# Four raw weight buffers in the first layer, a smaller descriptor reserve, and two conversion steps placed later

## The chip, the cores and the metric

The kernel runs on one core of a Trainium2 chip. The metric is device time in microseconds; the comparison is between medians of several runs. The core has a matrix engine (PE, with its weight loads shown as PEld), a vector engine (DVE), an activation engine (ACT), a general engine (POOL) and a sync engine (SP), which here issues all DMA transfers. Each engine works through its own instructions in order.

## What is computed

Three stages in float32, of which each feeds the next: causal attention with a decay, a layer with the activation h·cos(h), and a gated layer with silu.

```python
scores = scale * q @ k^T + (cum[:, None] - cum[None, :])   # causal, 32 heads of 576 x 64
x = softmax(scores) @ v                                    # then 2304 tokens x 512
h = x @ w_in;  x = (h * cos(h)) @ w_out                    # w_in 512 x 2048, w_out 2048 x 512
g = x @ w_gate; x = (silu(g) * (x @ w_val)) @ w_out2       # 512 x 1536, 1536 x 512
```

The five weight matrices arrive as float64 bit patterns (the kernel sees pairs of 32-bit words), so they have to be turned into float32 on the chip before a matmul can use them. A float32 operand is then split into a high and a low part, and three matmuls replace one.

## The kernel before

**Attention** runs over 16 pairs of heads. The order of its steps is written out by hand in the string `SCH`: each token is an operation and, behind the @, by how many rounds it lags. The loop of lines 626 to 630 walks through the string once a round and emits the operation for pair `n - lag`. `op` (line 551) changes the order for some pairs: `AHEAD` (line 567) lists operations that are emitted directly ahead of another one, and `BEHIND` keeps them from being emitted at their own place. `V0`, `V1` are the last matmuls of a pair, `N0`, `N1` the DVE products that normalise them (line 535), `xo` the DMA that stores the result (line 540), `lv` the DMA that loads values.

**Weight conversion** goes by blocks of 128x512 weights, 68 in all, listed in `order`; the first `SA` = 15 are converted during attention (one a pair), the other 53 during the first layer. `w_load(n)` has SP load the raw block, 512 KB, into a `wraw` tile (line 150). `w_step(n, k)` does one step: k = 1 is ACT's absolute value of the high words into a tile `ta` (line 166), k = 2 to 5 are four DVE operations (lines 168, 170, 172, 174), of which 4 and 5 read the raw block again; k = 6 makes the high part and k = 7, on POOL, the low part (line 113), for blocks below `SB` = 32. A later block, of the second layer, is joined with its neighbour in `w_member` (line 195): POOL makes four sums (line 207), ACT makes four high parts `hi` (line 225), POOL the four low parts (line 113), and SP stores all eight in DRAM (`put`, line 221). These twelve small jobs stand in the list `small` and are emitted one at a time.

**First layer.** The loop of lines 764 to 800 makes 96 steps; `in1` multiplies a chunk of 384 tokens by one block of w_in (12 matmuls, line 251) and forms h·cos(h): ACT rounds (line 661), DVE subtracts (663), ACT takes the sine (665), DVE multiplies (667), ACT makes the high part `gh` (669), DVE the low part `gl` (line 113). `out1` multiplies `gh` and `gl` by a block of w_out (12 matmuls, line 684), two steps later (`LAG`). The order inside a step is the string `ORD1`: digits are the parts of `in1`, w is a conversion step (`w_next`, line 702), c a small job, o is `out1`. The part 5 (`gh`) of a step is emitted in the following step. After the conversion's step 5 of block n, `w_next` emits step 1 of block n+1 and the load of block n + `RWB2` (line 714); the first `RWB2` loads are emitted at the layer's start (lines 775 to 777). The raw tiles come from the pool `stage2` (line 642), which holds `RWB2` of them. Near the end of a chunk the next chunk `xl` is loaded (line 265) and split by POOL in four parts (lines 116 and 113), one a step. A tiny DVE copy, `gate` (line 142), stands ahead of the load of the second chunk.

From line 762 on, the order of emission is the order on each engine; so it is in attention.

**Second layer** reads the stored weights (`u_read`, line 737) and is not touched by the change.

Of the kernel before, what the change touches and what calls it, by code (L numbers as in the profile page):

```python
# [20 lines left out]
NPAIR = NH // 2  # L21
# [15 lines left out]
WARM = 2  # L37
TAB = 2
TAB2 = 6
RWB2 = 2  # L40
HIB = 4
CHAIN = 1
WHE = 1
# [52 lines left out]
def body(ctx: ExitStack, tc: tile.TileContext, qk, v, f, w_in, w_out, w_gate, w_val, w_out2, mask_c, ident_c, sel_c, out):  # L96
    nc = tc.nc
# [48 lines left out]
    def w_load(n):  # L146
        kind, j = order[n]
        sp = stages[0] if n < SA else stages[1]
        raw = sp.tile([128, 512], I64, tag="wraw", name="wraw")
        SP.dma_start(out=raw, in_=srcs[kind][j])  # L150
        wcur[n] = [raw, None]
# [399 lines left out]
    def op(o, i):  # L551
# [9 lines left out]
        if (o, i) in BEHIND:  # L561
            return
        for a in AHEAD.get((o, i), ()):
            act(*a)
        act(o, i)

    AHEAD = {("M21", 1): (("ra", 0), ("rb", 0)), ("M00", 1): (("E20", 1),), ("C40", 0): (("E21", 1),)}
    BEHIND = {a for b in AHEAD.values() for a in b}

    def act(o, i):  # L570
        k, e = o[0], int(o[-1]) if o[-1] in "01" else 0
        p = 2 * i + e
        if o[:2] == "ld":
            i > 1 and load_pair(i)
        elif o == "lv":
            prep_v(i)
        elif k == "S":
            if i or o != "S1":
                emit_s(i, int(o[1]))
            if not i and o == "S3":  # L580
                emit_s(i, 1)
        elif k == "M":
            emit_m(p, int(o[1]))
        elif k == "E":
            emit_e(p, int(o[1]))
        elif k == "T":
            emit_t(i, int(o[1]), e)
        elif k == "C":
            emit_c(i, int(o[1]), e)
        elif k == "r":  # L590
            emit_recip(i, o[1])
        elif k == "V":
            emit_pv(i, e)
        elif k == "N":
            emit_n(i, e)
        elif o == "xo":
            emit_o(i)
        elif o == "xk":
            if i == XL:
                load_chunk(0, True)  # L600
            elif i >= XP:
                for _ in range(min(XN, len(xsplit))):
                    split_x(*xsplit.pop(0))
        elif o == "wd":
            i and w_load(i - 1)
        elif k == "w":
            i and w_step(i - 1, int(o[1]))
        elif o == "qb":
            emit_b(i)
        elif k == "q":  # L610
            i and emit_q(i, int(o[1]))
        else:
            raise ValueError(o)
# [27 lines left out]
    mp3 = lctx.enter_context(tc.tile_pool(name="mp3", bufs=3, reuse_waits="tile"))  # L641
    stages[1] = rctx.enter_context(tc.tile_pool(name="stage2", bufs=RWB2, side=SIDE_R))
    ps_h = hctx.enter_context(tc.tile_pool(name="ps_h", bufs=4, space=PSUM))
# [58 lines left out]
    def w_next():  # L702
# [8 lines left out]
        if SA < n <= SB and k in (3, 4):  # L711
            w_step(n - 1, k + 3)
        if k == 5 and n + RWB2 < len(order):
            w_load(n + RWB2)
        wpos[:] = (n + 1, 2) if k == 5 else (n, k + 1)
# [48 lines left out]
    for i in range(NCH + LAG):  # L764
        if i < NCH:
# [9 lines left out]
            if i == 0:  # L775
                for n in range(RWB2):
                    w_load(SA + n)
# [327 lines left out]
```

## Time and profile before

| what | value |
|---|---|
| median of 3 runs | 982.17 us (981.91 to 983.57) |
| the profiled execution | 981.45 us |
| its span, first to last instruction | 979.7 us |
| mean granted TensorE clock | 0.998 |
| busy: PE, DVE, ACT, POOL | 98%, 75%, 52%, 48% |
| stretch of attention; first layer; second layer | to about 170; to about 578; to the end |

The profile is of one execution. Times in rows are microseconds from the start of the span. A row of the timeline reads: start, length, engine and line, operation, written tile <- read tiles, form, count; in brackets the idle time of the engine just before and what ended it. SPq rows are DMA issues by SP; their length is that of the issue, not of the transfer. A wait for several things is put down to the last of them.

### The profile page before, as it was taken

How to read it: one execution, taken by the hardware profiler on the slowest of the kernel's cores; microseconds unless marked ns; L12 is line 12 of the kernel's file. 1: busy time of each engine (PE TensorE's matmuls, PEld its weight loads, DVE VectorE, ACT ScalarE, POOL GpSimd, SP SyncE). 2: the span in 40 equal slices, each digit the busy share in tenths (PEclk: the TensorE clock that was granted, in tenths of full speed). 3: DMA queues.
4: the chain of work that ended last, by engine and by line, in shares of the span. 5: the costliest groups of instructions: out<-in, count | busy, mean ns of one | idle time of the engine just before them, and what ended most of it. 6: DMA issues, size and time to landing. Idle time of an engine off the chain costs nothing.

```text
span 979.7 us, 17216 instructions
## 1 busy us (share of the span) xinstructions
PE 963.9 (98%) x6106; PEld 909.6 (93%) x6106; DVE 733.8 (75%) x1309; ACT 506.9 (52%) x1107; POOL 466.3 (48%) x493
## 2 busy tenths in 40 slices
PE   8999999999999999999989999999999999999998
PEld 5787887999999999989989999999999999988888
DVE  6988887887888768769875635756667585898884
ACT  7888886555555546546645531323233232464552
POOL 7787875422265586496783004455455455100000
PEclk9999999999999999999999999999999999999999
DMA  6666665433467857768857773325941329953431
GB/s 198 217 202 211 207 178 155 144 119 108 151 210 226 251 174 269 237 191 287 254 183 258 252 273 115 92 87 180 352 124 49 121 60 385 346 179 125 134 108 43
DMA packets 108981, 182.55 MB, mean 186 GB/s; under 512 B 8912, under 2 KB 72800, under 8 KB 108896
## 3 DMA queue, kind: packets, MB, share of 16 engines
q1 hardware_dynamic: 108896, 181.46, 57.0%
q8 instruction: 48, 0.79, 0.3%
q14 instruction: 37, 0.30, 0.1%
HBM read 118.43 MB, written 62.99 MB: 185 GB/s over the span
## 4 chain that ended last, share of the span: by engine, by line
PE 81%; POOL 5%; DMA 5%; DVE 4%; ACT 2%; issue 2%; SPq 0%; POOLq 0%; DVEq 0%; ACTq 0%
PE h L251 14%; PE t L684 12%; PE b L875 11%; PE c L875 8%; PE a L875 8%; PE b L964 5%; PE t L475 4%; PE t L526 4%; PE a L964 3%; DMA xl<-x 2%; PE sB L406 2%; PE sA L406 2%; PE sA L414 2%; PE c L964 2%; PE d L964 2%
## 5 line engine op out<-in xcount | busy, mean ns | idle before, releaser
L251 PE MATMUL h<-xh,w 128*128 128x384 f32 x768 | 148.9, 334 | 0.0
L684 PE MATMUL t<-gh,w 128*128 128x384 f32 x704 | 138.1, 337 | 8.6 <-ACT gh L669 8.5
L251 PEld LDWEIGHTS h<-xh,w 128*128 128x128 f32 x768 | 134.4, 188 | 0.2 <-issue 0.2
L684 PEld LDWEIGHTS t<-gh,w 128*128 128x128 f32 x704 | 123.9, 189 | 10.4 <-ACT gh L669 9.7
L875 PE MATMUL b<-c,wu 128*128 128x384 f32 x648 | 121.1, 334 | 0.0
L663 DVE SCALAR_TENSOR_TENSOR r<-h,n 128x384 f32<-128x384 f32 x96 | 53.2, 554 | 81.8 <-ACT n L661 81.5
L875 PEld LDWEIGHTS b<-c,wu 128*128 128x128 f32 x648 | 113.1, 188 | 0.0
L661 ACT ACTIVATE n<-h 128x384 int32<-128x384 f32 x96 | 47.0, 490 | 110.4 <-PE h L251 110.2
L838 POOL TENSOR_TENSOR s<-u,s 128x384 f32<-128x384 f32 x33 | 37.8, 1145 | 123.5 <-ACT s L837 110.8
L251 PE MATMUL h<-xl,w 128*128 128x384 f32 x384 | 82.3, 334 | 0.0
L875 PE MATMUL c<-c,wu 128*128 128x384 f32 x432 | 80.7, 334 | 0.0
L875 PE MATMUL a<-c,wu 128*128 128x384 f32 x432 | 80.7, 334 | 0.0
L684 PE MATMUL t<-gl,w 128*128 128x384 f32 x352 | 75.7, 336 | 0.0
L875 PEld LDWEIGHTS c<-c,wu 128*128 128x128 f32 x432 | 75.4, 188 | 0.0
L875 PEld LDWEIGHTS a<-c,wu 128*128 128x128 f32 x432 | 75.4, 188 | 0.0
L113 POOL TENSOR_TENSOR w<-ta,w 128x512 fp32r<-128x512 f32 x32 | 44.2, 1381 | 62.4 <-ACT w L188 30.8
L437 ACT ACTIVATE P<-P,mx 128x384 f32<-128x384 f32 (+3 forms) x128 | 70.3, 550 | 0.7 <-DVE mx L429 0.6
L166 ACT ACTIVATE ta<-wraw 128x512 f32<-128x512 f32 x68 | 45.9, 676 | 43.9 <-DMA wraw<-in_w_out_dram 23.6
L251 PEld LDWEIGHTS h<-xl,w 128*128 128x128 f32 x384 | 68.0, 188 | 0.2 <-issue 0.2
L174 DVE SCALAR_TENSOR_TENSOR ta<-wraw,ta 128x512 int32<-128x512 int32 x68 | 65.3, 960 | 0.5
L665 ACT ACTIVATE r<-r,hpi 128x384 f32<-128x384 f32 x96 | 59.5, 619 | 10.2 <-DVE r L663 9.7
L172 DVE SCALAR_TENSOR_TENSOR ta<-wraw,ta 128x512 int32<-128x512 int32 x68 | 63.9, 939 | 1.0
(153 smaller groups left out, 2076.3 us busy)
## 6 DMA issues: line engine op xcount, KB each, us to landing
wu<-wu SPq DMA_DIRECT2D x63, 512.0 KB, 6.5
wraw<-in_w_out_dram SPq DMA_DIRECT2D x28, 512.0 KB, 3.5
wu<-hi SPq DMA_DIRECT2D x54, 256.0 KB, 4.6
gd<-g SPq DMA_DIRECT2D x72, 192.0 KB, 2.4
gt<-gd SPq DMA_DIRECT2D x36, 384.0 KB, 4.9
raw<-in_qk_dram SPq DMA_DIRECT2D x16, 576.0 KB, 5.1
wu<-sums SPq DMA_DIRECT2D x36, 256.0 KB, 3.4
xb<-x SPq DMA_DIRECT2D x24, 384.0 KB, 7.4
```

The lines of the kernel that those rows point to most:

```text
L113: eng.tensor_tensor(out=o, in0=a, in1=b.bitcast(F32), op=ALU.subtract)
L166: ACT.activation(out=ta.bitcast(F32), in_=hi32, func=AF.Abs)
L172: DVE.scalar_tensor_tensor(out=ta, in0=lo, scalar=29, in1=ta, op0=ALU.logical_shift_right, op1=ALU.bitwise_or)
L174: DVE.scalar_tensor_tensor(out=ta, in0=hi, scalar=-(1 << 30), in1=ta, op0=ALU.bitwise_and, op1=ALU.bitwise_or)
L251: PE.matmul(ps, lhsT=w[:, a, 128 * kk:128 * kk + 128], rhs=b[:, kk], start=(n == 0), stop=(n == 3 * KD - 1))
L437: ACT.activation(out=o, in_=o, func=AF.Exp, scale=-1.0, bias=mxt[p % 8][:, t:t + 1], accum_out=smt[p // 2 % 3][:, c:c + 1])
L661: ACT.activation(out=n, in_=h, func=AF.Copy, scale=INV2PI, bias=0.25)
L663: DVE.scalar_tensor_tensor(out=r, in0=h, scalar=INV2PI, in1=n, op0=ALU.mult, op1=ALU.subtract)
L665: ACT.activation(out=r, in_=r, func=AF.Sin, bias=hpi, scale=float(2 * np.pi))
L684: PE.matmul(acc[m][:, :CH], lhsT=wo[:, q, 128 * m:128 * m + 128], rhs=x, start=(j == a and n == 0), stop=False)
L875: PE.matmul(d, lhsT=wu[q, i][1][:, mem, x, 128 * kt:128 * kt + 128], rhs=r, start=bool(s and n == 0), stop=(n == 5), skip_group_check=True)
L964: PE.matmul(ot[:, :w], lhsT=cmb[i][:, x, q], rhs=m[:, 256 * y:256 * y + w], start=(i in (1, 5) and n == 0), stop=(n == len(ops) - 1), skip ...
```

## The change

It has three parts. The pool of the first layer holds four raw blocks instead of two, so four are loaded at the start of the layer, and each later load is emitted two blocks earlier. To make room for these 8 KB a partition, the reserve that the program keeps for descriptors of dynamic transfers goes from 16 KB to 4 KB a partition. And in the next to last round of attention, the conversion steps 4 and 5 of the last block that attention converts (pair 15) are emitted directly ahead of step 7 of the block before, that is behind `N1` and `N0` of pair 14 and not ahead of them.

```diff
-RWB2 = 2
+RWB2 = 4
...
-    AHEAD = {("M21", 1): (("ra", 0), ("rb", 0)), ("M00", 1): (("E20", 1),), ("C40", 0): (("E21", 1),)}
+    AHEAD = {("M21", 1): (("ra", 0), ("rb", 0)), ("M00", 1): (("E20", 1),), ("C40", 0): (("E21", 1),),
+             ("w7", NPAIR - 2): (("w4", NPAIR - 1), ("w5", NPAIR - 1))}
...
-    nc = _bacc.Bacc("TRN2", target_bir_lowering=False, num_devices=1)
+    nc = _bacc.Bacc("TRN2", target_bir_lowering=False, num_devices=1, dynamic_dma_scratch_size=4096)
```

## Rows read from the trace of the kernel before

**Rows 1.** The profile's page: busy time; queues with packets, MB, share; one issue line

```profile
PE 963.9 (98%) x6106; PEld 909.6 (93%) x6106; DVE 733.8 (75%) x1309; ACT 506.9 (52%) x1107; POOL 466.3 (48%) x493
...
q1 hardware_dynamic: 108896, 181.46, 57.0%
q8 instruction: 48, 0.79, 0.3%
q14 instruction: 37, 0.30, 0.1%
...
wraw<-in_w_out_dram SPq DMA_DIRECT2D x28, 512.0 KB, 3.5
```

**Rows 2.** Waits of PE, 150 to 580: who, for whom; us, times, longest

```profile
PE t L684 <- ACT gh L669: 8.5, 4, 3.1
```

**Rows 3.** Timeline of PE, first layer: starts of blocks of `in1`

```profile
330.96 1.55 PE L251 MATMUL h<-xh,w 128*128 128x384 f32 x8
335.12 1.55 PE L251 MATMUL h<-xh,w 128*128 128x384 f32 x8
...
372.20 1.56 PE L251 MATMUL h<-xh,w 128*128 128x384 f32 x8
...
422.16 1.55 PE L251 MATMUL h<-xh,w 128*128 128x384 f32 x8
430.52 1.55 PE L251 MATMUL h<-xh,w 128*128 128x384 f32 x8
...
501.84 1.55 PE L251 MATMUL h<-xh,w 128*128 128x384 f32 x8
...
513.56 1.55 PE L251 MATMUL h<-xh,w 128*128 128x384 f32 x8
```

**Rows 4.** Timeline of ACT, first layer: step 1 of a block behind its raw load

```profile
354.53 0.67 ACT L166 ACTIVATE ta<-wraw 128x512 f32<-128x512 f32 x1 [5.69 <-DMA wraw<-in_w_gate_dram]
...
425.30 0.67 ACT L166 ACTIVATE ta<-wraw 128x512 f32<-128x512 f32 x1 [5.55 <-DMA wraw<-in_w_val_dram]
```

**Rows 5.** Timeline of SP's issues ahead of the first of these steps

```profile
349.90 0.36 SPq L221 DMA_DIRECT2D wu<-ta  x1
350.36 0.42 SPq L150 DMA_DIRECT2D wraw<-in_w_gate_dram  x1
```

**Rows 6.** Timeline of POOL behind the loads of two later chunks

```profile
345.43 0.52 POOL L116 TENSOR_SCALAR xh<-xl 128x384 fp32r<-128x384 f32 x1 [5.76 <-DMA xl<-x]
...
350.54 0.51 POOL L116 TENSOR_SCALAR xh<-xl 128x384 fp32r<-128x384 f32 x1
...
358.06 1.07 POOL L207 TENSOR_TENSOR sums<-ta,sums 128x256 f32<-128x256 f32 x1
...
360.99 0.92 POOL L207 TENSOR_TENSOR sums<-ta,sums 128x256 f32<-128x256 f32 x1
...
485.21 0.52 POOL L116 TENSOR_SCALAR xh<-xl 128x384 fp32r<-128x384 f32 x1 [2.65 <-DMA xl<-x]
...
496.80 0.74 POOL L207 TENSOR_TENSOR sums<-ta,sums 128x256 f32<-128x256 f32 x1
```

**Rows 7.** Timeline of DVE, SP, ACT and PE where attention ends

```profile
164.81 1.38 DVE L174 SCALAR_TENSOR_TENSOR ta<-wraw,ta 128x512 int32<-128x512 int32 x1
166.11 0.81 DVE L535 TENSOR_TENSOR xp<-t,rs 128x320 f32<-128x320 f32 x2
...
170.99 0.33 SPq L540 DMA_DIRECT2D x<-xp  x1
...
175.14 0.14 DVE L142 CAST xl<-gs 1x1 fp32r<-1x1 f32 x1 [0.54 <-DMA x<-xp]
...
175.79 0.48 ACT L669 CAST gh<-h 128x384 fp32r<-128x384 f32 x1
...
179.03 1.55 PE L684 MATMUL t<-gh,w 128*128 128x384 f32 x8
```

**Rows 8.** DMA rate, 168 to 181, in 40 slices of 0.325 us

```profile
GB/s 369 277 28 0 0 0 13 88 63 202 391 416 429 403 403 403 373 398 418 135 0 0 0 0 0 0 104 85 109 312 402 397 406 392 203 10 0 0 0 0
```

## The prediction

> **What bounds the kernel now.** I read the page first: PE is busy for 963.9 of 979.7 us [rows 1]. An edit that removes no matmul can win only where PE stands still, or runs below its usual pace. So the second view was PE's waits in the first layer, where the raw buffers are used: four waits, all of the matmul of `out1` for ACT's `gh`, 8.5 us in total, 3.1 us the longest [rows 2]. Idle time is not all that is lost, since PE can also be slow after a wait, so I took the loss from PE's own pace. Undisturbed, one `in1` block follows the last after 335.12 - 330.96 = 4.16 us [rows 3]. Against that pace:
> - from 330.96 to 372.20 there are nine periods: 41.24 - 9 x 4.16 = 3.80 us lost;
> - from 422.16 to 430.52 there is one: 8.36 - 4.16 = 4.20 us lost, more than the idle time, since the matmuls behind this wait ran slowly;
> - from 501.84 to 513.56 there are two: 11.72 - 8.32 = 3.40 us lost.
>
> Together 11.4 us, all [rows 3]. Why was `gh` late? ACT's timeline shows ACT itself standing still ahead of `w_step` 1 for 5.69 us and 5.55 us, until the raw block landed [rows 4]; the other two waits look alike. ACT works in order, so the rounding `n` and `gh` of the layer are queued behind that step. PE forgives the first 3.6 us (5.69 less a mean wait of 8.5 / 4 = 2.1) [rows 2, 4]: `gh` is used two steps later.
>
> And why is the raw block late? SP's issues show it. The load that ACT awaits at 354.53 was issued at 350.36, right behind a store of `ta` at 349.90 [rows 5]; that store waits for a low part by POOL, and POOL had stood still for 5.76 us until the next chunk `xl` had landed at 345.43 [rows 6]. So the chain is: chunk load, POOL, store, SP's queue, raw load, ACT, PE. With two buffers, a raw load is emitted one block ahead of its use, so any delay in SP's queue goes straight into ACT.
>
> **The change part by part.**
>
> *Four raw buffers.* No operation, transfer or byte is added; the load of block n+4 stands where that of n+2 stood, and waits for the same event, that block n is read for the last time. SP's queue and what is queued behind on it stay as they were. A block now has three block times instead of one to arrive. One block time is at least 4/3 of a step (three conversion parts a step, four to a block), so the two more give at least 2 x 4/3 x 4.16 = 11 us (the step from [rows 3]). The waits shown are under 6 us [rows 4], and none of the four cost PE over 3.1 us [rows 2], so none was over 3.1 + 3.6 = 6.7 us. All four waits of ACT for raw blocks end: gain 11.4 us.
>
> What is late next? POOL, for it is still 5.8 us behind [rows 6], and ACT soon needs its sums. In the first place POOL works without a break from 345.43; the third sum of the next pair ends at 358.06 + 1.07 = 359.13 [rows 6], and ACT's high part of the sums stands behind it, with `n` and `gh` behind that. But in this stretch DVE had stopped too, since it waits for ACT, and POOL may be slower beside a busy DVE. One row pair bounds this: the same POOL work, from the second quarter of the chunk split to the fourth sum, took 360.99 + 0.92 - 350.54 = 11.37 us here, and 496.80 + 0.74 - 485.21 = 12.33 us at the third place, where DVE ran [rows 6]. That is 0.96 us more; with as much again for the part before, by half, I take 1.4. Then the sum ends at 360.5; ACT adds the high part, `n` and `gh`, about 1.4 us (three operations of about 0.48, as in [rows 7]): 361.9. PE would need that `gh` when it ends the block that starts at 335.12 + 6 x 4.16 = 360.08, that is 2.08 later, at 362.2. It fits, by 0.3 us. I charge 0.1 us for all three places, with 0 below and the rival's 5.0 above.
>
> *The start of the layer.* Two more loads, 1.05 MB, are issued ahead of the store of the last attention result (170.99), and the gate on DVE waits for that store (175.14) [rows 7]. The DMA rate in this stretch was about 400 GB/s while both loads and the store ran, then zero [rows 8]: 1.05 MB take 2.6 us more. So the gate ends at about 177.8 instead of 175.14, and `gh`, which ended 1.13 us after the gate's start (175.79 + 0.48), at 178.9, against its use at 179.03 [rows 7]. With up to 0.5 us from the moved steps it is late by 0.4: I charge 0.4 us, with 0 below. Above: were each load alone as slow as 3.5 us [rows 1], the gate would come 7.0 us later, and `gh` at 183.3, 4.3 us late.
>
> *The moved steps.* `w4` and `w5` of the last block change places with `N1` and `N0`, which took 0.81 us behind a `w5` of 1.38 us [rows 7]. The same DVE work in another order; it issues no DMA. `N` now comes up to 2 x 1.38 us earlier, and its store with it, which nothing awaits; the block's low part on POOL, and the four raw loads that wait for it, come up to 0.8 us later. I take 0.5, counted above. If DVE meets `N` before PE is through, the two steps wait with it; that is within the same 0.8. Below: up to 1 us gained, if the order at the seam lets PE start sooner.
>
> *The reserve.* The trace shows three queues, one hardware_dynamic and two for instructions [rows 1], none filled by software, and all issues in the rows are SP's. I charge nothing; the other end is the last rival. The Trainium skill, page "DMA: Bandwidth & Descriptors", section "SWDGE vs HWDGE vs iDMA", says that transfers issued from SP have their descriptors made in hardware and never touch the ring in SBUF; by it this part costs nothing, and the queue list agrees as far as it goes.
>
> **Sum.** 981.45 - 11.4 + 0.1 + 0.4 = 970.55 us for the profiled execution. That execution was 0.72 us below the median of 982.17, so the median should be 971.3 us.
>
> **The rivals.**
>
> *POOL takes the place of the raw load.* If POOL suffers more from DVE than the row pair says, ACT waits longer for the sums. For it: POOL has no slack behind a chunk load, and the margin above is only 0.3 us. Against: the pair of rows differs by 0.96 us only. The price: were POOL slower three times as much as I took, 4.2 us instead of 1.4, `gh` would be late by 2.5 us at the first place; at the second about the same; the third, where DVE ran beforehand, little. That is 5.0 us in place of 0.1: 976.2. Were the matmuls slow behind one of these waits too, as behind the one at 422.16 (4.20 lost, of which 5.55 - 3.6 = 1.95 idle [rows 3, 4]), 2.2 us more. The Trainium skill, page "SBUF — State Buffer", section "Who interferes with whom", gives a rule on this side: DVE operations with two SBUF inputs and POOL operations that read SBUF exclude each other, and the later one waits for the whole of the first. The rows agree in sign (12.33 against 11.37) and say how much of it this mix shows.
>
> *The burst of loads at the seam* costs its upper price, 4.3 us instead of 0.4: 975.2. Against it: 400 GB/s with two loads in flight [rows 8].
>
> *The change doesn't do what it says.* A wait is put down to whatever ended last; if ACT's step waited as long for its `ta` tile, nothing moves: 982. Against it: the load issued at 350.36 plus 3.5 us to land and some latency is just 354.5 [rows 1, 4, 5], and there are six `ta` tiles.
>
> *Slower: the smaller reserve throttles SP's transfers.* If SP's descriptors were kept there, a quarter of the room would allow fewer transfers in flight. The place is every stretch with many transfers, the second layer's weight reads above all. The price: 181.46 MB go through SP's queue [rows 1]; one load at a time moves 524 KB in 3.5 us, 150 GB/s, which is 1210 us. It decides once the rate that is left falls below 181.46 MB / 971 us = 187 GB/s; a milder throttle, felt only at peaks, would give some 985 to 1000.
>
> **How the numbers follow.** Forecast, 969.3 to 973.5 us: chance 0.66. POOL rival, 973.5 to 978.5: 0.15. Seam rival: 0.07. No effect: 0.05. Slower: 0.07. The low end is the full 11.4 us, no charge, 1 us from the seam and 0.5 of scatter between runs: 969.3. The high end takes in the seam rival and the POOL rival up to 5 us: 976.8. A measurement of this kernel can tell a difference of about 0.2%, 2 us, from none. Faster by more than that: 0.66 + 0.15 + 0.07 = 0.88; same 0.05; slower 0.07.
>
> **What would show it.** Right: no wait of ACT for `wraw` over 1 us after 290; no wait of PE for `gh` in the first layer; a new wait of ACT's high part for POOL's sums of some 2 to 4 us at the three chunk loads; `in1` blocks 4.16 us apart throughout; the granted clock at full level there. At the seam, a later gate on DVE and the same busy time in attention. Wrong: PE still waits for `gh`, with ACT behind POOL (the POOL rival) or behind the gate (the seam rival); or longer transfers everywhere (the reserve).

## The result and the profile after

The changed kernel takes 972.49 us (median of 4 runs, 971.26 to 974.82), the kernel before, beside it, 982.87 (981.91 to 984.76): a ratio of 0.9895 with a 95% interval of 0.987 to 0.992. The profiled execution took 972.01 us with a span of 970.2; the one of before 981.45 with 979.7. The forecast was 971.3 (969.3 to 976.8), faster. Line numbers behind 567 are one higher in the changed kernel: L684 is now L685, L669 L670.

The page of the changed kernel, busy time and the shares of the chain that ended last (compare [rows 1]; in the chain of before PE had 81%, POOL and DMA 5% each):

```profile
PE 960.5 (99%) x6106; PEld 907.6 (94%) x6106; DVE 740.5 (76%) x1309; ACT 505.4 (52%) x1107; POOL 468.9 (48%) x493
...
PE 89%; DVE 3%; DMA 2%; ACT 2%; POOL 2%; issue 1%; SPq 0%; DVEq 0%; POOLq 0%; ACTq 0%
```

The work is the same. PE's idle time fell from 15.8 to 9.7 us, and its busy time by 3.4 us, since the same matmuls ran slowly for less time; part of that is the clock, told below. ACT's waits from 260 to 510 in the changed kernel (who waits, for whom: us in total, times, longest) show the cause:

```profile
ACT n L662 <- PE h L251: 76.4, 49, 2.3
ACT gh L670 <- DVE h L668: 17.4, 15, 2.1
ACT hi L225 <- POOL sums L207: 7.7, 3, 4.3
...
```

No step `ta <- wraw` waits for its DMA here any longer; the waits of 5.69 and 5.55 us [rows 4] are gone. In their place stands the high part `hi` behind POOL's sums, three times. PE's waits from 150 to 580 in the changed kernel, against the 8.5 us of [rows 2]:

```profile
PE t L685 <- ACT gh L670: 1.2, 2, 0.9
PE t L685 <- ACT ta L166: 1.2, 1, 1.2
PE t L688 <- DVE gl L113: 0.6, 1, 0.6
...
```

So PE still loses something, in two places. The starts on PE's timeline in the changed kernel say where (undisturbed, `in1` blocks are 4.16 us apart [rows 3]):

```profile
169.77 1.55 PE L251 MATMUL h<-xh,w 128*128 128x384 f32 x8
176.01 1.55 PE L251 MATMUL h<-xh,w 128*128 128x384 f32 x8
179.15 1.68 PE L685 MATMUL t<-gh,w 128*128 128x384 f32 x8 [0.89 <-ACT gh L670]
181.36 1.55 PE L251 MATMUL h<-xh,w 128*128 128x384 f32 x8
...
426.80 1.55 PE L251 MATMUL h<-xh,w 128*128 128x384 f32 x8
431.24 1.57 PE L251 MATMUL h<-xh,w 128*128 128x384 f32 x8
...
436.02 1.55 PE L251 MATMUL h<-xh,w 128*128 128x384 f32 x8
...
441.10 1.55 PE L251 MATMUL h<-xh,w 128*128 128x384 f32 x8
444.51 1.62 PE L685 MATMUL t<-gh,w 128*128 128x384 f32 x8 [1.17 <-ACT ta L166]
446.67 1.55 PE L251 MATMUL h<-xh,w 128*128 128x384 f32 x8
...
563.15 1.03 PE L251 MATMUL h<-xh,w 128*128 128x384 f32 x5
```

From 176.01 to 181.36 are 5.35 us, 1.19 too many: the start of the layer. From 426.80 to 446.67 are 19.87 us for four periods, 3.23 too many: behind the second of the three chunk loads that the prediction looked at. Elsewhere the pace holds.

From the row at 169.77, the second block start of the layer, to the last one at 563.15 are 393.38 us; in the kernel before, between the same two blocks, 401.09 (170.71 to 571.80). Undisturbed this stretch takes 389.2 (the version `both4` below shows 389.25), so before lost 11.9 us in it and after 4.2. This "loss in the layer" is the measure used below, since it leaves out what varies ahead of the layer and behind it. Of the 9.5 us by which the span fell, 7.7 are this loss; 0.94 is that PE began the layer earlier, and 0.84 fell behind the layer, which the change does not touch. The last two change from one profile to the next without a change of code (the part behind the layer was 407.0 and 407.9 us in two profiles of one version), so they are not credited to the change.

### The profile page after: what moved, and what is told of

Same layout as the page of the kernel before. It is cut to its first block, busy times and chain, and to the rows that moved or that the text cites. A ratio compares the mean times of both kernels' runs of the same rounds, so it can differ in the third digit from the quotient of the medians.

```text
span 970.2 us, 17227 instructions
## 1 busy us (share of the span) xinstructions
PE 960.5 (99%) x6106; PEld 907.6 (94%) x6106; DVE 740.5 (76%) x1309; ACT 505.4 (52%) x1107; POOL 468.9 (48%) x493
## 4 chain that ended last, share of the span: by engine, by line
PE 89%; DVE 3%; DMA 2%; ACT 2%; POOL 2%; issue 1%; SPq 0%; DVEq 0%; POOLq 0%; ACTq 0%
PE h L251 18%; PE t L685 17%; PE b L876 12%; PE c L876 8%; PE a L876 8%; PE b L965 5%; PE t L526 4%; PE t L475 4%; PE a L965 3%; PE sB L406 2%; PE sA L414 2%; PE sA L406 2%; PE c L965 2%; PE d L965 2%; PE t L688 2%
## 5 line engine op out<-in xcount | busy, mean ns | idle before, releaser
L685 PE MATMUL t<-gh,w 128*128 128x384 f32 x704 | 136.5, 335 | 2.4 <-ACT gh L670 1.2
L685 PEld LDWEIGHTS t<-gh,w 128*128 128x128 f32 x704 | 123.1, 188 | 3.4 <-ACT gh L670 1.8
L685 PE MATMUL t<-gl,w 128*128 128x384 f32 x352 | 75.3, 334 | 0.0
L685 PEld LDWEIGHTS t<-gl,w 128*128 128x128 f32 x352 | 62.2, 188 | 0.3 <-DVE gl L113 0.3
```

Source lines behind the costliest of these rows:

```text
L685: PE.matmul(acc[m][:, :CH], lhsT=wo[:, q, 128 * m:128 * m + 128], rhs=x, start=(j == a and n == 0), stop=False)
```

## The experiments

All ratios are to the kernel before, run beside it on the same chip, with 95% intervals. "Loss" is that of the layer, from one profile each. "Gate" is how long after the second block start the gate on DVE started.

| kernel | median us | ratio | loss us | gate us |
|---|---|---|---|---|
| before | 982.87 | 1 | 11.9 | 4.43 |
| changed | 972.49 | 0.9895 [0.987, 0.992] | 4.2 | 8.20 |
| raw4: four buffers and the small reserve | 973.13 | 0.9909 [0.9878, 0.994] | 4.7 | 7.85 |
| raw3: changed, with three buffers | 974.64 | 0.9916 [0.9889, 0.9943] | 4.2 | 8.03 |
| moved: the two steps alone | 981.98 | 0.9997 [0.9977, 1.0018] | 16.0 | 6.82 |
| reserve: the small reserve alone | 982.38 | 1.0011 [0.999, 1.0032] | 15.5 | 5.61 |
| hold4: changed, chunk split later | 971.62 | 0.9906 [0.9886, 0.9926] | 1.4 | 8.40 |
| stag4: changed, two loads later | 972.40 | 0.991 [0.989, 0.9931] | 2.2 | 6.88 |
| both4: hold4 and stag4 | 969.82 | 0.989 [0.9867, 0.9912] | 0.1 | 6.44 |
| hold2: before, chunk split later | 970.17 | 0.989 [0.9871, 0.9908] | 1.5 | 5.63 |
| hold1: before, split one step later | 970.99 | 0.9893 [0.9868, 0.9918] | 1.0 | 4.55 |

### The parts one at a time

**raw4** is the kernel before with the buffers and the reserve, without the moved steps.

```diff
-RWB2 = 2
+RWB2 = 4
-    nc = _bacc.Bacc("TRN2", target_bir_lowering=False, num_devices=1)
+    nc = _bacc.Bacc("TRN2", target_bir_lowering=False, num_devices=1, dynamic_dma_scratch_size=4096)
```

> Four raw buffers and the small reserve, the two conversion steps left at their old place. Theory (the raw loads that come in time are the whole gain): ACT never waits over 1 us for wraw, ratio to the kernel before 0.988 to 0.991. Rival (the moved steps carry part of it, for PE starts the first layer 0.94 us earlier in the changed kernel): PE waits 0.7 us for the values' DMA as before, and the ratio is 0.991 to 0.993.

**moved** is the kernel before with the moved steps alone.

```diff
+             ("w7", NPAIR - 2): (("w4", NPAIR - 1), ("w5", NPAIR - 1))}
```

> The two conversion steps moved, with two raw buffers and the old reserve. Theory: ratio 0.999 to 1.001, the four waits of ACT for wraw of over 4 us stay. Rival (the move counts): PE's values wait at the end of attention is gone, ratio 0.998 to 0.999.

**raw3** is the changed kernel with one buffer less.

```diff
-RWB2 = 4
+RWB2 = 3
```

> The changed kernel with three raw buffers, so a load has two block times (about 11 us) and not three. Theory (a raw load is late by one stand of POOL, 6 to 7 us, and no more): the waits for wraw are under 1 us, ratio 0.987 to 0.991, and the gate at the start of the layer is about 1.3 us earlier than with four. Rival (the delay needs both blocks): some waits of 1 to 4 us stay, ratio 0.992 to 0.996.

**reserve** is the kernel before with the small reserve alone.

```diff
-    nc = _bacc.Bacc("TRN2", target_bir_lowering=False, num_devices=1)
+    nc = _bacc.Bacc("TRN2", target_bir_lowering=False, num_devices=1, dynamic_dma_scratch_size=4096)
```

> The kernel before with the small reserve alone. Theory: ratio 0.999 to 1.001, landing times of the transfers unchanged. Rival (transfers throttled): over 1.002, with longer landing times.

The buffers carry the whole gain; the other two parts alone change nothing that can be measured. ACT's waits from 260 to 510 say the same. First moved:

```profile
ACT ta L166 <- DMA wraw<-in_w_out_dram: 19.9, 8, 6.9
```

then raw4, where no line for `wraw` stands at all:

```profile
ACT hi L225 <- POOL sums L207: 13.9, 7, 4.2
```

and raw3:

```profile
ACT hi L225 <- POOL sums L207: 9.4, 5, 3.7
ACT ta L166 <- DMA wraw<-in_w_val_dram: 0.5, 1, 0.5
```

With two buffers ACT waits for the raw block; with three or four it waits for POOL. The third buffer takes the raw wait down to 0.5 us; the fourth brings no time that can be measured (0.9916 and 0.9895, with intervals that overlap; 0.991 at most was expected of raw3).

Two more expectations were missed here. The gate of raw3 came 8.03 us behind the second block start and not 1.3 us earlier than with four. SP's issues in the changed kernel show why:

```profile
170.62 0.34 SPq L150 DMA_DIRECT2D wraw<-in_w_in_dram  x1
...
171.48 0.43 SPq L150 DMA_DIRECT2D wraw<-in_w_in_dram  x1
172.01 0.38 SPq L540 DMA_DIRECT2D x<-xp  x1
172.43 0.49 SPq L150 DMA_DIRECT2D wraw<-in_w_out_dram  x1
```

The fourth load stands behind the store that the gate waits for, so it was never ahead of it. And with the moved steps alone the gate came 6.82 us behind the block start, some 1.2 to 2.4 later than the 4.4 to 5.6 of unmoved kernels with two loads, where the prediction had 0.8 at most. In the changed kernel a copy `gs <- rs` that waits for a DMA stands ahead of the last `w5` on DVE, the low part on POOL follows it, and the first raw load is issued only then, at 170.62. DVE's timeline in the changed kernel (compare the 164.81 of [rows 7]):

```profile
167.78 0.14 DVE L634 COPY gs<-rs 1x1 f32<-1x1 f32 x1 [0.81 <-DMA rs<-r_d]
167.85 0.67 DVE L174 SCALAR_TENSOR_TENSOR ta<-wraw,ta 128x512 int32<-128x512 int32 x1
...
177.97 0.14 DVE L142 CAST xl<-gs 1x1 fp32r<-1x1 f32 x1 [4.31 <-DMA x<-xp]
```

For the reserve, the ratio of 1.0011 is a little past the expected 0.999 to 1.001; its interval, 0.999 to 1.0032, takes in the 1.002 of the run's rival, but hardly the 985 us and more (1.003 and more) of the prediction's. The median landing of the second layer's weight reads was 7.1 us with the small reserve alone against 6.5 before. But over all profiles it lies between 5.8 and 6.5 with the old reserve and between 6.1 and 7.5 with the small one; whether the reserve lengthens it a little is left open. The time shows nothing of it that can be measured.

### POOL's stand, with four buffers and with two

The waits of ACT that remain go back to POOL, which stands still until the next chunk has landed. **hold4** is the changed kernel with POOL's split of a chunk not begun before two steps after its load, so that POOL goes on with its sums until then.

```diff
+    hold = [XS]
...
                 load_chunk(c + 1, later=True)
+                hold[0] = max(XS, i + 2)
...
-            if xsplit and i >= XS:
+            if xsplit and i >= hold[0]:
```

> The changed kernel with the same delay of the splits. Theory (the 3.2 us still lost at 427 to 447 come from POOL's lag behind the chunk load): they go, no wait of ACT for sums over 1 us, ratio 0.985 to 0.988. Rival (DVE, busy without a break there, is the bound): PE still loses 2 us or more there, ratio 0.988 to 0.990.

**hold2** is the same edit on the kernel before, with its two buffers and its reserve.

> The kernel before, two raw buffers, but POOL begins to split a chunk two steps after the chunk's load is emitted, so that it does not stand still for the chunk. Theory (the raw loads were late because POOL stood still and SP's queue stood behind it): the waits of ACT for wraw of over 4 us go, though there are two buffers, ratio 0.989 to 0.993. Rival (two buffers are too few in themselves, one block time being too short for a load): those waits stay, ratio over 0.997.

In hold4 ACT has no wait for sums left at all, and the periods at the second chunk load are 4.16 us each but for 0.12 us. Its loss fell to 1.4, of which 1.36 stand at the start of the layer. The ratio, 0.9906, missed what was expected, and can't be told from the changed kernel's: the loss at the start stayed, and in its profile PE began the layer 1.65 us later than in `both4` (172.36 against 170.71), ahead of all that was edited. In that profile the granted clock stood at 0.51, its lower level, from 18.2 to 21.6 us, early in attention; half of these 3.4 us is as much as the late start. So the gain of hold4 is shown in its trace and not in its time.

hold2 tells most. Its waits of ACT from 260 to 510:

```profile
...
ACT ta L166 <- DMA wraw<-in_w_out_dram: 12.6, 8, 3.2
ACT ta L166 <- DMA wraw<-in_w_val_dram: 4.9, 4, 3.3
```

and SP's issue of the load that stood at 350.36 in [rows 5]:

```profile
342.62 0.36 SPq L221 DMA_DIRECT2D wu<-ta  x1
343.75 0.35 SPq L150 DMA_DIRECT2D wraw<-in_w_gate_dram  x1
```

With two buffers and no stand of POOL, the raw load is issued 6.6 us earlier. ACT still waits for raw blocks, but 3.3 us at most, which is less than the 3.6 us that the prediction had PE forgive. The loss falls from 11.9 to 1.5, and the kernel is as fast as the changed one or faster. So the whole chain from the chunk load over POOL, the store and SP's queue to the raw load was the cause: the buffers bridge it, the later split takes it away.

DVE is a rival to POOL as the cause of the loss at the second chunk load, for it has no pause there. Two windows of ten us show changed and then hold4 (columns: busy us of PE, PEld, DVE, ACT, POOL with counts, granted clock, DMA share, GB/s):

```profile
430.00:440.00 10.00, 9.06 (x49) 8.14 (x48) 9.90 (x15) 5.85 (x13) 9.77 (x9) 1.00 0.82 263
440.00:450.00 10.00, 8.83 (x52) 8.54 (x51) 9.96 (x16) 5.91 (x13) 8.57 (x9) 1.00 0.92 307
```

```profile
430.00:440.00 10.00, 10.00 (x59) 9.84 (x58) 9.71 (x15) 5.56 (x12) 9.68 (x10) 1.00 0.82 259
440.00:450.00 10.00, 10.00 (x60) 10.00 (x59) 9.24 (x16) 6.50 (x14) 9.21 (x9) 1.00 0.82 283
```

DVE and POOL are nearly as busy in hold4, and PE has no pause. A busy DVE alone is thus not what stops PE. Nor is it ACT's wait alone; stag4 shows both below.

### The start of the layer

**stag4** is the changed kernel with the third and fourth of the first loads issued at step 3.

```diff
-                for n in range(RWB2):
+                for n in range(2):
+                    w_load(SA + n)
+            if i == 3:
+                for n in range(2, RWB2):
                     w_load(SA + n)
```

> The changed kernel with the third and fourth raw load emitted at step 3 of the layer and not at its start. Theory (the burst of four loads delays the last attention store and so the gate): the gate on DVE waits under 1.5 us instead of 4.3, PE's wait of 0.9 us there goes, 1.0 to 1.2 us gained, ratio 0.987 to 0.989. Rival (the gate is late because the moved steps make the first load late): the gate still waits over 3 us, nothing gained.

**both4** has both edits, hold4 and stag4.

> The changed kernel with both the delayed splits and the later third and fourth load. Theory: both gains add up, ratio 0.984 to 0.987. Rivals as for the two alone: 0.988 or more.

In stag4 the gate waited 3.00 us, where under 1.5 was expected; the moved steps still delay the first load. The ratio, 0.991, missed the expected 0.987 to 0.989 as well. PE lost nothing at the start all the same, and the loss of 2.2 us stands at the second chunk load alone. Its timeline of DVE and PE:

```profile
177.60 0.14 DVE L142 CAST xl<-gs 1x1 fp32r<-1x1 f32 x1 [3.00 <-DMA x<-xp]
...
179.04 1.55 PE L685 MATMUL t<-gh,w 128*128 128x384 f32 x8
```

The gate's start is only 0.37 us earlier than in the changed kernel; PE's second block is 0.95 us later there (170.72 against 169.77). So only the distance counts. (A late start of PE doesn't shorten it by itself: hold4 and raw3 began later still, with the gate at 8.40 and 8.03.) Over the profiles, with the gate 6.88 us or less behind the second block start nothing was lost; at 7.85, 8.03, 8.20 and 8.40 it was 0.79, 1.0, 1.19 and 1.36 us. Each is what the distance exceeds 7.0 us by, to within 0.06.

stag4 also tells what sets the price of ACT's wait for POOL. At the first and at the second of the three chunk loads ACT was held just as long, and came free at the same point of PE's period, 3.89 us behind a block start (355.84 and 422.42):

```profile
359.73 0.62 ACT L225 CAST hi<-sums 128x512 fp32r<-128x512 f32 x1 [3.24 <-POOL sums L207]
...
426.31 0.62 ACT L225 CAST hi<-sums 128x512 fp32r<-128x512 f32 x1 [3.25 <-POOL sums L207]
```

PE lost nothing behind the first and 2.4 us behind the second. Both waits are under 3.6 us, so that figure doesn't divide them. DVE does. It worked without a pause behind both, and its product `h` came at these times, behind the first wait and behind the second:

```profile
365.03 0.55 DVE L668 TENSOR_TENSOR h<-h,r 128x384 f32<-128x384 f32 x1
...
367.90 0.55 DVE L668 TENSOR_TENSOR h<-h,r 128x384 f32<-128x384 f32 x1
...
371.78 0.55 DVE L668 TENSOR_TENSOR h<-h,r 128x384 f32<-128x384 f32 x1
...
431.61 0.55 DVE L668 TENSOR_TENSOR h<-h,r 128x384 f32<-128x384 f32 x1
...
435.64 0.55 DVE L668 TENSOR_TENSOR h<-h,r 128x384 f32<-128x384 f32 x1
...
439.91 0.56 DVE L668 TENSOR_TENSOR h<-h,r 128x384 f32<-128x384 f32 x1
...
444.64 0.55 DVE L668 TENSOR_TENSOR h<-h,r 128x384 f32<-128x384 f32 x1
```

At the first place a step of the layer cost DVE 2.87 and 3.88 us, less than PE's 4.16, so it caught up; at the second 4.03, 4.27 and 4.73 us, so it fell further back. The program's text says why: `WQ` gives a step three conversion parts and the next one two while the blocks of w_gate and w_val are converted, and three in every step from the first block of w_out2 on, which begins just behind the second place. hold4 has that pace too and lost 0.12 us there, since ACT was not held. So by these profiles it takes both, a stand of ACT and a DVE without room. No run changed `WQ`: that the pace sets the price is read from the trace and the program's text, and not tried.

In the loss both4 is the sum of both: 0.1 us and no wait of PE for `gh`, `gl` or ACT in the layer. Its ratio, 0.989, missed the expected 0.984 to 0.987 and lies where its rival had it. From 170.71 to 559.96 are 389.25 us on PE's timeline:

```profile
170.71 0.69 PE L251 MATMUL h<-xh,w 128*128 128x384 f32 x3
...
559.96 0.85 PE L251 MATMUL h<-xh,w 128*128 128x384 f32 x4
```

### Again, with more runs

The ratios so far don't tell these versions from the changed kernel. To see whether they are ahead of it, four ran on one chip: the changed kernel, both4 and hold2 unedited, and **hold1**, which is hold2 with `i + 1` in the place of `i + 2`.

> The changed kernel again, on one chip with the three below. Theory: ratio to the kernel before 0.988 to 0.992, 3 to 5 us lost in the first layer, most of it at about 427 to 447 behind a wait of ACT for POOL's sums of 3 to 5 us.

> The kernel before, two raw buffers, with the splits one step later in place of two, so that POOL stands 4.2 us less behind a chunk load and 2 us or so are left. Theory (POOL's stand reaches PE through SP's queue and the raw load, and PE forgives 3.6 us): the waits of ACT for wraw fall to under 4 us, little of the 11 to 16 us lost in the first layer is left, ratio 0.988 to 0.992. Rival (a stand of any length stops SP's queue long enough): waits of 4 us and more at the chunk loads, ratio over 0.994.

> Two raw buffers and splits two steps later, again beside the changed kernel. Theory: 0.988 to 0.990, 1 to 3 us faster than the changed kernel. Rival: the same as the changed kernel within 1 us.

> Four raw buffers, later splits, third and fourth load later, again beside the others. Theory: under 0.5 us lost in the first layer, 0.986 to 0.989, 3 to 4 us faster than the changed kernel. Rival: no faster than the kernel with two buffers and later splits.

| kernel | median us | runs | ratio | loss us |
|---|---|---|---|---|
| changed | 973.61 | 971.81 to 975.37 | 0.9919 [0.9895, 0.9943] | 4.1 |
| hold1 | 970.99 | 969.66 to 971.92 | 0.9893 [0.9868, 0.9918] | 1.0 |
| hold2 | 970.36 | 969.62 to 973.35 | 0.9891 [0.9867, 0.9916] | 0.9 |
| both4 | 969.52 | 968.55 to 969.78 | 0.9877 [0.9849, 0.9905] | 0.1 |

The loss of the changed kernel is at the same two places again (1.08 us at the start, the rest from 431 to 447), with ACT's waits for sums at 3.25 and 4.12 us. both4 is the fastest, and its runs do not overlap with those of the changed kernel. hold1 and hold2 can't be told apart, and hold2 is not told from both4 for sure. With two buffers and one edited condition, hold2 is as near to the best as the runs can say.

## Why the prediction was right, and where it was not

**The raw waits (forecast: 11.4 us gained).** Right, in size and in mechanism. Every wait for a raw block over 1 us is gone, and raw4 shows the whole gain without the moved steps. By all periods the loss of before was 11.9 us. It isn't a fixed figure: the three profiles with two buffers and the early split lost 11.9 (before), 15.5 (reserve) and 16.0 us (moved). Part of that is the clock. In moved, behind a wait of PE of 3.81 us, the granted clock stood at half, the 1.2 GHz level, for 6.8 us, and at full level on either side:

```profile
507.90:514.70 6.80, 6.23 (x19) 6.23 (x20) 5.57 (x10) 3.78 (x8) 3.23 (x4) 0.50 0.37 125
```

In before it stood at 0.50 for 3.4 us from 426.9, which are the slow matmuls that the prediction noted behind its second wait. With the waits gone, so is this.

**POOL (forecast: 0.1 us, shown: 3.2).** This is the term that was mis-sized. The mechanism was named, and at the first place it was worked out well: the third sum was to end at 360.5 and ended at 359.65, the same POOL work took 11.61 us against 11.37 [rows 6], ACT's `hi` waited 1.99 us, and PE lost nothing. The step that failed was "I charge 0.1 us for all three places": the first place's margin was taken for the second, where ACT was held longer and DVE had no room to catch up. POOL's and ACT's timelines in the changed kernel, first place and second, show the difference:

```profile
345.18 0.51 POOL L116 TENSOR_SCALAR xh<-xl 128x384 fp32r<-128x384 f32 x1 [5.37 <-DMA xl<-x]
...
358.91 0.74 POOL L207 TENSOR_TENSOR sums<-ta,sums 128x256 f32<-128x256 f32 x1
...
412.87 0.51 POOL L116 TENSOR_SCALAR xh<-xl 128x384 fp32r<-128x384 f32 x1 [6.49 <-DMA xl<-x]
...
426.62 0.73 POOL L207 TENSOR_TENSOR sums<-ta,sums 128x256 f32<-128x256 f32 x1
```

```profile
359.68 0.62 ACT L225 CAST hi<-sums 128x512 fp32r<-128x512 f32 x1 [1.99 <-POOL sums L207]
...
427.38 0.62 ACT L225 CAST hi<-sums 128x512 fp32r<-128x512 f32 x1 [4.34 <-POOL sums L207]
```

From the chunk's landing to the end of the sum POOL took 14.5 us both times. But the first chunk landed 0.76 us ahead of ACT's next rounding (345.94), the second 0.37 us behind it (412.50), and from there ACT came to `hi` 1.2 us sooner (10.5 us in place of 11.7). So ACT waited 4.34 us: 0.7 more than the 3.6 that the prediction had PE forgive. But that excess is the lesser part. In stag4 a wait of 3.25 us, under 3.6, cost 2.4 us at the same place, as DVE's steps there took longer than PE's period; hold4 takes the wait of ACT away and 3.1 of the 3.2 us with it. The working of the prediction has no row of DVE's work a step, at either place. The third place cost nothing, as expected; POOL stood 2.36 us there. The margin of the first place is no fixed figure either: in the second profile of the changed kernel `hi` waited 3.25 us there, and PE lost 0.2 us; in raw4, where `hi` waited 3.24 us and, 11 us earlier, 2.00 us, PE lost 1.0 us.

So the rival of POOL came about in part: its mechanism at one place of two, with 3.2 of its 5.0 us, and not because POOL was slower beside DVE. Some of DVE's operations were slower there. The conversion step of line 170 in the stretch 428 to 450, by form (times, busy us, mean ns), first in the changed kernel and then in hold4:

```profile
L170 DVE TENSOR_SCALAR ta<-ta 128x512 int32<-128x512 int32 x4 | 4.2, 1052 | 0.0
```

```profile
L170 DVE TENSOR_SCALAR ta<-ta 128x512 int32<-128x512 int32 x4 | 2.5, 629 | 0.0
```

In before it took 486 ns in the same stretch, where POOL was busy too but DVE had pauses. Other steps went the other way: line 174 took 1001 ns in the changed kernel and 1282 in hold4. The four DVE steps of a block together (their means in this stretch, added up) took 3.72 us in the changed kernel, 3.38 in hold4, 3.35 in before and 3.83 in hold2, which lost 0.6 us there. So slower operations on DVE alone don't explain the 3.2 us. The Trainium skill, page "SBUF — State Buffer", section "Who interferes with whom", says that an operation of the kind of line 170 (a `tensor_scalar`) can hold the port pair that DVE and POOL share, and that whichever engine issues first blocks the other. The trace agrees in kind: this one DVE operation is about twice as long, while POOL's whole stretch grew by 0.24 us only. No run here took POOL away from beside DVE, so that the pair of ports is the cause is argued and not shown.

**The start of the layer (forecast: 0.4 us, shown: 1.2).** The gate was forecast for 177.8, or 178.3 with the moved steps, and came at 177.97; but that agreement is luck, since PE began the layer 0.94 us earlier. Counted from the second block start, the gate was to come 2.7 to 3.2 us later than in before and came 3.8 later (8.20 against 4.43), and it is this distance that PE's loss follows. The parts of the forecast were wrong in both directions: the moved steps alone cost the gate 1.2 to 2.4 us in place of 0.5, and the loads, with the reserve, some 2.2 to 3.4 (7.85 of raw4 less the same 4.4 to 5.6) where 2.6 was forecast; together they came to less than the sum of both, and there the fourth load stands behind the store.

**The reserve and the moved steps** cost nothing that can be measured, as forecast. The run speaks against the rival that the smaller reserve throttles SP's transfers: 1.0011, with at most 1.0032 in its interval.

**What would show it.** Two of the signs were wrong: PE still waits for `gh` (0.9 us at the start, 0.3 at the second place, there beside 0.6 for `gl` and 1.2 for an ACT step of the conversion), and the blocks are not 4.16 us apart throughout. They are those of the two mis-sized terms.

**The sum.** The two terms came out 3.9 us worse together (3.2 and 1.2 for 0.1 and 0.4), yet the median is only 1.2 us above the forecast. The rest is no merit of the working. Of the 9.5 us by which the profiled span fell, 1.8 lie outside the layer's loss and are not credited to the change; that is luck. The medians of the two sets differ by 10.4 and 8.8 us. both4, which lost 0.1 us, ran 11.6 and 12.9 us under before in its two sets, so the usual loss of before is about 12 to 13 us: an estimate, which takes the rest of the kernel as equal. Less the 4.2 of the changed kernel that is some 7.5 to 8.8 us. The second set meets it; the first, whose interval is 7.9 to 12.8 us (0.992 to 0.987), takes it in at its lower end.

## What to carry to other kernels

When an engine that works in order stands on a load, look at what queues behind it: here one early split of a chunk held POOL, POOL held a store, the store held SP's queue, and a weight load two stages on came late. More buffers bridge such a stand and pass the wait on to the next engine that it feeds; starting the landed tile's work later takes it away, and gave at least as much here with half the buffers. And when one stall recurs at several places, price each place by its own rows, and with them those of the engine that has to catch up: the same wait of 3.2 us cost nothing where DVE's steps took 2.9 to 3.9 us of a period of 4.16, and 2.4 us where they took 4.0 to 4.7.

## What the runs showed of the hardware

- The same DVE operation on 128x512 int32 took 486 (before), 629 (hold4) and 1052 ns (changed) on average from 428 to 450, with POOL busy for 16.0, 18.9 and 18.3 of the 20 us from 430 to 450. The step of line 174 took 1034, 1282 and 1001 ns there, so a single line's mean doesn't tell how slow DVE is.
- The granted clock halved for 3.4 to 6.8 us behind some waits of PE and not behind others of the same kernel: in before behind one of 2.36 us, and not behind one of 3.06 us. What tells them apart stays open.
- Two-buffer kernels of nearly the same code lost 11.9 to 16.0 us in the same stretch, so the profile of one execution gives such a loss only to within 4 us. The times of the kernel before, in its runs beside the others, went from 976.8 to 985.5 us.
